# Seven block products for eight in the first MLP layer of the second pass

## The chip, the cores and the metric

The kernel runs on one core of a Trainium2 chip. The metric is device time in microseconds. A row or bar named PE is TensorE, DVE is VectorE, ACT is ScalarE, POOL is GpSimd and SP is the engine that issues nearly all transfers here.

## The reference

2048 tokens of width 640 are normalised, and two branches are added to the input: linear attention with a learned feature map (32 heads of 20), and an MLP that normalises once more.

```python
xn = _layernorm(x, axis=-1)
return x + _A_ref(xn, A_wqkv, A_w_phi, A_wo) + _B_ref(xn, B_w1, B_b1, B_w2, B_b2)

def _B_ref(x, w1, b1, w2, b2):
    y = _layernorm(x, axis=-1)
    h = _gelu(jnp.einsum("bsd,df->bsf", y, w1) + b1)      # 640 -> 1728
    return jnp.einsum("bsf,fd->bsd", h, w2) + b2          # 1728 -> 640
```

In the attention branch q and k go through a small matrix per head and two softmaxes (of p and of -p), `kv` and `z` are sums over all tokens, and the output is `(phi_q kv) / (phi_q z)`, projected by `wo`.

## The kernel before

Everything is float32. Each operand of a large product is split into a high part, which is the value rounded by a copy to `float32r`, and a low part, which is the rest. A product then takes three matmuls, high by high, high by low and low by high (`mm3`, lines 69 to 72). A split is one copy on ScalarE (line 61) and one subtraction on VectorE or POOL (line 64).

Activations lie turned: features on the 128 partitions, tokens along a row. The 2048 tokens are four blocks of 512. The 640 inputs are five slices of 128 (`KC`), the 1728 hidden features fourteen chunks of 128, the last one half full. Two chunks make a group `g`, seven groups in all.

The program has these stages on PE:

1. The first MLP pass, over blocks 0 and 1. Beside its matmuls a generator (`prep`) prepares the attention weights, and then normalises blocks 2 and 3 slice by slice and writes their high and low parts to DRAM (`y_dram`).
2. The projections of q, k and v for 16 tiles of 128 tokens, with the feature map on ScalarE, VectorE and POOL, and the sums `kv` on PE (to about 443 us of the trace).
3. The second MLP pass, over blocks 2 and 3, from there to about 648 us. Beside it a generator (`attend`) computes the attention output: it loads features `e`, splits them (ScalarE copy, POOL subtraction, lines 960 and 961), has PE multiply them with `kv` (lines 967 and 968), and puts the two halves of a bank together (lines 977 and 978). When a block is through, `quotients` brings the denominators into place and POOL multiplies by their reciprocals (line 1013).
4. The output projection, and its sum with the MLP result.

In a pass, `Mlp.passes(g, b, ws)` computes for a group and a block: for each of its two chunks five `mm3` into one PSUM bank (15 matmuls), gelu on ScalarE, high and low part of the result; then, after a `yield`, five rows of second products, each of two `mm3` into one of three banks, which VectorE adds to `acc[b]` (line 309). The second products of one group and block stand behind the first products of the next.

PE's order is written out by hand. What runs beside is interleaved by a call after each `mm3`, which advances the generator by one step:

```python
mm3(pz, w[0][:, kc, :], w[1][:, kc, :], y[b][0][:, kc, :], y[b][1][:, kc, :], kc == 0, kc == KC - 1)
next(self.beside, None)
```

In the second pass from group 1 on, the order on VectorE, ScalarE and POOL is the order of the program text too. Before that a scheduler sets it. An engine works through its queue in order, and a waiting instruction holds up those behind it. SP issues transfers in order in the same way.

The weights of a chunk are loaded to `r1` (of w1) and `r2` (of w2), split into one of four tiles `w0` to `w3`, and the next chunk is loaded when the split is through.

Of the kernel before, what the change touches and what calls it, by code (L numbers as in the profile page):

```python
# [51 lines left out]
def tile_kernel(ctx: ExitStack, tc: tile.TileContext, x, xT, wkT, wqT, wv, wphi, wo, w1, b1, w2, b2,  # L52
# [24 lines left out]
    ones1 = cp.tile([1, P], F32, name="ones1")  # L77
# [4 lines left out]
    rs_all = cp.tile([P, 16], F32, name="rs_all")  # L82
    nc.vector.memset(ones1, 1.0)
# [7 lines left out]
    r_dram = {n: tc.dram_tile([n, 8, P], F32, name=f"r{n}") for n in (1, 2)}  # L91
    a_dram = [tc.dram_tile([P, KC, 512], F32, name=f"a{b}") for b in range(2)]
# [108 lines left out]
    def load_rows(b):  # L201

        mr = mtile(5)
# [7 lines left out]
    class Mlp:  # L211
        def __init__(self, slots, hid):
            self.hid, self.turn, self.slots, self.beside, self.raw = hid, 0, slots, iter(()), {}
            self.ph, self.px, self.po = Banks(0, 1, 2), Banks(3, 4), Banks(5, 6, 7)

# [40 lines left out]
        def first(self, g, j, b, w, gt, hh, hl):  # L256
            pz = self.ph()
            for kc in range(KC):
                mm3(pz, w[0][:, kc, :], w[1][:, kc, :], y[b][0][:, kc, :], y[b][1][:, kc, :], kc == 0, kc == KC - 1)
                next(self.beside, None)  # L260
# [6 lines left out]
        def passes(self, g, b, ws, hid=None):  # L267
# [27 lines left out]
            for m in range(KC):  # L295
                pw = self.po()
                ms = slice(m * P, (m + 1) * P)
                for j, (hh, hl) in enumerate(hid):
                    w2h, w2l = ws[j][2:]
                    if hl is not None:  # L300
                        mm3(pw, w2h[:, ms], w2l[:, ms], hh, hl, j == 0, j == 1)
                        next(self.beside, None)
# [5 lines left out]
                else:  # L308
                    nc.vector.tensor_tensor(acc[b][:, m, :], pw, acc[b][:, m, :], op=ALU.add)  # L309

# [230 lines left out]
    def prep():  # L541
# [13 lines left out]
        mr = load_rows(2)  # L555
# [6 lines left out]


        def load(b, c):
            xc = fp.tile([P, D], F32, name="raw")[:, :512]
            nc.sync.dma_start(xc, xT[c * P:(c + 1) * P, b * 512:(b + 1) * 512])
            return xc

        for b in range(2, 4):
            ahead = load(b, 0)  # L570
            if b == 3:
                mr = load_rows(3)
            for _ in range(5 if b == 2 else 10):
                yield
            for c in range(KC):
                xc, ahead = ahead, load(b, c + 1) if c < KC - 1 else None
                nc.gpsimd.tensor_tensor(xc, xc, mr[:, 0], op=ALU.subtract)
                for _ in range(3):
                    yield
                nc.vector.tensor_tensor(xc, xc, mr[:, 1], op=ALU.mult)  # L580
                for _ in range(2):
                    yield
                hl = fp.tile([P, 2, KC, G5], F32R, name="t").rearrange("p a c f -> p a (c f)")[:, :, :512]
                nc.scalar.activation(hl[:, 0], xc, AF.Copy)
                for _ in range(2):
                    yield
                nc.vector.tensor_tensor(hl[:, 1], xc, f(hl[:, 0]), op=ALU.subtract)
                for p in range(2):
                    nc.sync.dma_start(y_dram[b - 2][p][:, c, :], f(hl[:, p]))
                yield  # L590
# [193 lines left out]
    for t, i in [(t, i) for t in range(14) for i in range(4)] + TAIL:  # L784
# [35 lines left out]
        if (t, i) == (11, 0):  # L820
            mlp = Mlp((0, 3, 2, 1), ((1, 2), (0, 3)))
            mlp.ph = ptile
            mlp.fetch(0)
        if (t, i) == (12, 3):
            with tc.issue_after(evac):
                ws = [mlp.take(0)]
            mlp.fetch(1)
        if (t, i) == (15, 3):
            w, late = mlp.take_parts(1)
            ws.append(w)  # L830
# [3 lines left out]
    mlp.fetch(2)  # L834
    wkv.close()

# [6 lines left out]
    kvs = bp.tile([P, 11, P], F32R, name="kvs")  # L843
    fs = ExitStack()
# [20 lines left out]
    load_acc(3)  # L865

# [10 lines left out]
    def finish_kv(pxt):  # L877
# [9 lines left out]
        def done(tp, dens, mask, hi, lo):  # L887
# [3 lines left out]
            km = sp.tile([G6, 5, VR], F32, name="km", bufs=2)[:r, :n, :w]  # L891
# [25 lines left out]
    class Attention:  # L917

        def __init__(self, b, bank):
            self.b, self.n, self.bank = b, 0, bank  # L920
            self.ob = op.tile([P, KC, 512], F32, name=f"ob{b}") if b < 2 else acc01.tile([P, KC, 512], F32, name=f"acc{b - 2}")
# [12 lines left out]
        def groups(self, wait, first, gaps, lag):  # L934
# [16 lines left out]
            for p in late:  # L951
                self.second(*p)
                yield
                yield

        def first(self, g):
# [4 lines left out]
            nc.gpsimd.tensor_tensor(pl, e, f(ph), op=ALU.subtract)  # L961
            return ph, pl

        def second(self, g, ph, pl):
# [13 lines left out]
            nc.vector.tensor_tensor(o, pn[a, :], t, op=ALU.add)  # L978
            if g == 10:
                nc.sync.dma_start(o_dram[self.b], o[0:40])  # L980
# [134 lines left out]
    for _ in before:  # L1115
        pass
# [83 lines left out]
```

## Time and profile before

| | |
|---|---|
| time, median of 3 runs | 721.05 us (720.82 to 721.19) |
| span of the profiled execution, from its first to its last instruction | 719.3 us |
| median less that span | 1.75 us |
| busy: PE, DVE, ACT, POOL | 710.7, 477.6, 323.0, 384.1 us |
| DMA | 91.88 MB, mean 128 GB/s |

The profile comes from one execution; the page gives its span, and the table the distance to the runs' median. Instructions that only wait or issue transfers are not counted as busy. PE's matmuls overlap, so that a row of 0.39 us can stand 0.23 us after the one before it. The name on the left of an arrow is the tile written, those on the right the tiles read. In brackets stands how long the engine was idle before, and what ended that.

### The profile page before, as it was taken

To read this page: it belongs to the slowest core of one execution; us is meant where nothing else is said; L and a number is where in the kernel's file an instruction comes from. 1 tells how busy PE (TensorE), PEld (TensorE's weight loads), DVE (VectorE), ACT (ScalarE), POOL (GpSimd) and SP (SyncE) were. 2 spreads that over 40 slices of the span, in tenths; PEclk is the share of its full clock that TensorE was granted. 3 is DMA by queue.
4 is the path that set the end of the run, shared out by engine and by line. 5 is a ranking of instruction groups with operands and counts; after the bars stand their busy time and mean duration, and the time that the engine had idled before them with its cause. 6 is when DMAs were issued, how large, how long until landed. Compare 5 with 4: busy or idle time off the path is not lost.

```text
span 719.3 us, 9640 instructions
## 1 busy us (share of the span) xinstructions
PE 710.7 (99%) x3411; PEld 598.2 (83%) x3411; DVE 477.6 (66%) x787; ACT 323.0 (45%) x530; POOL 384.1 (53%) x332
## 2 busy tenths in 40 slices
PE   8989999999999999999999999999999999999998
PEld 7868888888888888888888887888888888888887
DVE  7776754757554788788898887635565566766432
ACT  6434454334334544545435446346565556530200
POOL 3521223345045997897878879346577787403000
PEclk9999999999999999999999999999999999999999
DMA  9803642656411227326302506943443443164122
GB/s 328 264 8 109 195 133 84 179 158 192 139 74 73 92 82 232 85 97 214 80 0 55 130 3 204 229 144 111 135 128 127 134 153 94 49 230 132 74 87 74
DMA packets 60454, 91.88 MB, mean 128 GB/s; under 512 B 7014, under 2 KB 31366, under 8 KB 59038
## 3 DMA queue, kind: packets, MB, share of 16 engines
q1 hardware_dynamic: 60102, 91.25, 40.7%
q8 instruction: 27, 0.44, 0.2%
q14 instruction: 21, 0.17, 0.1%
q10 hardware_dynamic: 304, 0.01, 0.0%
HBM read 63.51 MB, written 27.73 MB: 127 GB/s over the span
## 4 chain that ended last, share of the span: by engine, by line
PE 87%; DVE 3%; POOL 3%; ACT 1%; issue 1%; DMA 0%; SPq 0%; POOLq 0%
PE bank L673 23%; PE bank L70 18%; PE bank L72 18%; PE bank L71 18%; PE bank L743 2%; PE bank L499 2%; POOL m L708 2%; PE bank L967 1%; PE bank L968 1%; POOL m L719 1%; PE bank L305 1%; PE bank L285 1%; PE bank L304 1%; PE bank L286 1%; DVE sm L711 1%
## 5 line engine op out<-in xcount | busy, mean ns | idle before, releaser
L673 PE MATMUL bank<-wkh,y 128*128 128x512 f32 (+1 forms) x480 | 139.5, 364 | 0.0
L64 POOL TENSOR_TENSOR w<-r,w 128x640 fp32r<-128x640 f32 x52 | 83.3, 1619 | 95.6 <-ACT w L61 64.7
L70 PE MATMUL bank<-y,w 128*128 128x512 f32 (+1 forms) x334 | 129.8, 389 | 1.0 <-ACT m L264 1.0
L71 PE MATMUL bank<-y,w 128*128 128x512 f32 (+1 forms) x334 | 129.2, 387 | 0.0
L72 PE MATMUL bank<-y,w 128*128 128x512 f32 (+1 forms) x334 | 129.2, 387 | 0.0
L70 PE MATMUL bank<-m,w 128*128 128x512 f32 x260 | 102.4, 394 | 2.6 <-DVE acc L309 2.3
L72 PE MATMUL bank<-m,w 128*128 128x512 f32 x260 | 101.3, 389 | 0.0
L71 PE MATMUL bank<-m,w 128*128 128x512 f32 x260 | 101.2, 389 | 0.0
L673 PEld LDWEIGHTS bank<-wkh,y 128*128 128x128 f32 x480 | 87.5, 188 | 13.3
L309 DVE TENSOR_TENSOR acc<-bank,acc 128x512 f32<-128x512 f32 x120 | 81.1, 684 | 19.8 <-PE bank L72 11.8
L673 PE MATMUL bank<-wkl,y 128*128 128x512 f32 (+1 forms) x240 | 87.4, 364 | 0.0
L64 DVE TENSOR_TENSOR m<-m,m 128x512 fp32r<-128x512 f32 (+1 forms) x54 | 43.7, 814 | 65.5 <-ACT m L61 65.3
L70 PEld LDWEIGHTS bank<-y,w 128*128 128x128 f32 x334 | 62.7, 188 | 13.9 <-ACT m L264 1.2
L72 PEld LDWEIGHTS bank<-y,w 128*128 128x128 f32 x334 | 62.7, 188 | 12.8
L71 PEld LDWEIGHTS bank<-y,w 128*128 128x128 f32 x334 | 62.7, 188 | 12.5
L264 ACT ACTIVATE m<-bank,b1t 128x512 f32<-128x512 f32 (+1 forms) x54 | 36.2, 671 | 65.2 <-PE bank L72 61.0
L709 ACT ACTIVATE m<-m,rs_all 128x1280 f32<-128x1280 f32 x32 | 43.7, 1365 | 42.9 <-POOL m L708 42.9
L70 PEld LDWEIGHTS bank<-m,w 128*128 128x128 f32 x260 | 48.8, 188 | 14.4 <-DVE acc L309 3.5
L961 POOL TENSOR_TENSOR e<-e,m 128x512 fp32r<-128x512 f32 x28 | 36.2, 1295 | 41.8 <-ACT m L960 35.8
L711 DVE TENSOR_REDUCE sm<-m 128x64 f32<-128x1280 f32 x32 | 47.4, 1481 | 15.5 <-ACT m L709 15.4
L673 PE MATMUL bank<-w,y 128*128 128x512 f32 x240 | 57.4, 391 | 0.0
L72 PEld LDWEIGHTS bank<-m,w 128*128 128x128 f32 x260 | 48.8, 188 | 10.3
(156 smaller groups left out, 1249.3 us busy)
## 6 DMA issues: line engine op xcount, KB each, us to landing
r<-in_w SPq DMA_DIRECT2D x52, 320.0 KB
e<-e SPq DMA_DIRECT2D x40, 256.0 KB
e<-acc SPq DMA_DIRECT2D x52, 160.0 KB
acc<-in_xT SPq DMA_DIRECT2D x4, 1280.0 KB
xb<-in_x SPq DMA_DIRECT2D x8, 320.0 KB
t<-in_x SPq DMA_DIRECT2D x8, 320.0 KB
raw<-in_xT SPq DMA_DIRECT2D x10, 256.0 KB
yh<-t SPq DMA_DIRECT2D x10, 256.0 KB
```

The source lines that it names most:

```text
L64: eng.tensor_tensor(lo, src, f(hi), op=ALU.subtract)
L70: nc.tensor.matmul(ps, lh, rh, start=first, stop=False, **kw)
L71: nc.tensor.matmul(ps, lh, rl, start=False, stop=False, **kw)
L72: nc.tensor.matmul(ps, ll, rh, start=False, stop=last, **kw)
L264: nc.scalar.activation(gt, pz, AF.Gelu_apprx_tanh, bias=b1t[:, 2 * g + j:2 * g + j + 1])
L309: nc.vector.tensor_tensor(acc[b][:, m, :], pw, acc[b][:, m, :], op=ALU.add)
L499: nc.tensor.matmul(ps[:, u * nh * DF:(u + 1) * nh * DF], raw[:nh * DH, u * P:(u + 1) * P], wpt[:nh * DH, g, :nh, 1:], start=True, stop=True)
L673: nc.tensor.matmul(ps, lh[:, kc, c], rh[:, kc], start=n == 0, stop=n == 3 * KC - 1)
L708: subs[n, t] = nc.gpsimd.tensor_tensor(ep[:, s], a, b, op=ALU.subtract)
L709: exps[n, t] = nc.scalar.activation(e, e, AF.Exp, scale=rs_all[:, t:t + 1])
L711: nc.vector.tensor_reduce(sm, e.rearrange("p s (h f) -> p (s h) f", f=DH), axis=AX, op=ALU.add)
L961: nc.gpsimd.tensor_tensor(pl, e, f(ph), op=ALU.subtract)
```

## The change

For groups 1 to 5 of the second pass, the first products of a pair of chunks and of blocks 2 and 3 are computed together. Two chunks by two slices on the left, and two slices by two blocks on the right, are a 2 x 2 by 2 x 2 product of blocks; Strassen's method in Winograd's form takes seven products instead of eight. Slices 0 and 1 are one such product, slices 2 and 3 the other; slice 4 is computed as before (`rest`). Groups 0 and 6 stay as they were.

The weights' sums (`s1`, `s2`, `s4`, and `s3` in the place of a21) are computed by POOL in float32 and split: the rows and `s` go through ScalarE; the low part of `s` is subtracted on VectorE. The sums and differences of blocks 2 and 3 are computed in `prep` during the first pass, on POOL, and stored to `t_dram`; `t2`, `t3` and `t4` come back to two tiles `tf`, and `t1` takes the place of slices 0 and 2 of block 3, `y[3]`. The products gather in three banks; the four results are copied out of a bank by ScalarE, and VectorE adds another bank to each.

```diff
+        def cross(self, g, bs, before, later):
...
+            product("a", "a11", "b11", True)
+            copy(z11, "a")
+            product("c", "a12", "b21", True)
+            rest("c", 0, b0)
+            add(z11, "c")
+            hidden(z11, 0, hid[0][0])
+            next(before)
+            later[0]()
+            product("b", "s1", "t1", True)
+            copy(z22, "b")
+            product("a", "s2", "t2")
+            copy(z12, "a")
+            next(before)
+            later[1]()
+            next(before)
+            product("a", "s3", "t3")
+            copy(z21, "a")
+            bank["c"] = banks.tile([P, 512], F32, name="bank2")
+            product("c", "a22", "t4", True)
+            rest("c", 1, b0)
+            add(z21, "c")
+            hidden(z21, 1, hid[0][1])
+            product("b", "s4", "b22")
+            rest("b", 0, b1)
+            add(z12, "b")
+            self.after(2, lambda: gelu(z12, 0))
+            next(before)
+            later[2]()
+            rest("a", 1, b1)
+            add(z22, "a")
+            self.after(2, lambda: gelu(z22, 1))
+            for _ in before:
+                pass
```

Here `product` is two `mm3` (slices 2q and 2q + 1 of a block), `next(before)` is one row of the second products of the group before, and `later` are the splits of this group's w2 and the sums of the next group's w1. The second products of block 2 follow, with the splits of the next group's w1 beside their first three rows.

The weights are now loaded and split in other pieces: both chunks of w1 of a group, then both of w2, through the same two tiles `r1` and `r2`.

```diff
+        def sums(self, g):
...
+            for out, x0, x1, op in ((s[:, 0], a21, a22, ALU.add), (a21, a11, a21, ALU.subtract),
+                                    (s[:, 1], s[:, 0], a11, ALU.subtract), (s[:, 2], a12, s[:, 1], ALU.subtract)):
+                nc.gpsimd.tensor_tensor(out, x0, x1, op=op)
```

Steps are put off. The call after each `mm3` is now `tick`, which first issues what has come due and then advances the generator. With it the low part of a weight or of `e` is issued one tick after its high part, the add of attention's two halves two ticks after the copy, and gelu two ticks after the add.

```diff
+        def tick(self):
+            self.ticks += 1
+            while self.due and self.due[0][0] <= self.ticks:
+                self.due.pop(0)[2]()
+            next(self.beside, None)
...
-            nc.gpsimd.tensor_tensor(pl, e, f(ph), op=ALU.subtract)
+            mlp.after(1, lambda: nc.gpsimd.tensor_tensor(pl, e, f(ph), op=ALU.subtract))
```

At the start of the second pass two loads of `tf` (1.6 MB each) and four loads of `t1` into `y[3]` are added; after group 5, slices 0 and 2 of `y[3]` are loaded again. Space is found by keeping the attention output of all blocks in the tiles `acc0` and `acc1`: blocks 0 and 1 are written to DRAM after the multiplication and loaded back for the output projection.

```diff
+    for q in range(2):
+        nc.sync.dma_start(f(tf[q]), t_dram[q][:, 1:4])
...
-            self.ob = op.tile([P, KC, 512], F32, name=f"ob{b}") if b < 2 else acc01.tile([P, KC, 512], F32, name=f"acc{b - 2}")
+            self.ob = acc01.tile([P, KC, 512], F32, name=f"acc{b % 2}")
...
+                    if self.b < 2:
+                        nc.sync.dma_start(ob_dram[self.b][:, c - 1], ob[:, c - 1])
```

A small constant tile is shortened, another (`pad`) added, and a scratch area shortened, so that the tiles that one instruction reads and writes start at the same address modulo 64.

More of the change, by code (lines that the diff above doesn't have):

```diff
@@ L1115, in tile_kernel @@
-    for _ in before:
-        pass
+    nothing = iter(())
+    mlp.beside = finish_kv(mlp.px)
+    with tc.issue_after(subs["q", 15].ins):
+        mlp.sums(1)
+    this = mlp.passes(0, 3, ws)
+    next(this)
+    finish(before)
+    before = this
+    for q in range(2):
+        for p in range(2):
+            nc.sync.dma_start(f(y[3][p][:, 2 * q]), t_dram[q][:, 0, p])
+    mlp.places()
+    for part in mlp.splits(1):
+        part()
+        mlp.tick()
+    mlp.tick()
+    mlp.fetch_pair(1, True)
@@ new lines, in tile_kernel @@
+    for g in range(1, 6):
+        w2t, later = gathered(g)
+        hid, more = mlp.cross(g, (2, 3), before, later)
+        if g < 5:
+            parts = mlp.splits(g + 1)
+        else:
+            w1t, parts = mlp.take_pair(6, False, 1)
+        for m, _ in enumerate(mlp.second(g, 2, w2t, hid[0])):
+            next(more, None)
+            if m < len(parts):
+                parts[m]()
+            if m == 3:
+                mlp.fetch_pair(g + 1, True)
+        before = mlp.second(g, 3, w2t, hid[1])
@@ L1119, in tile_kernel @@
+    finish(before)
     pw_ = Banks(6, 7)
```

301 lines of the change are left out of this document (220 added, 81 removed).

## The prediction

> **What bounds the kernel now.** I read the page first, then the busy time by stretches, then the second pass in order of time.
>
> ```profile
> PE 710.7 (99%) x3411; PEld 598.2 (83%) x3411; DVE 477.6 (66%) x787; ACT 323.0 (45%) x530; POOL 384.1 (53%) x332
> PEclk9999999999999999999999999999999999999999
> PE 87%; DVE 3%; POOL 3%; ACT 1%; issue 1%; DMA 0%; SPq 0%; POOLq 0%
> ```
>
> TensorE is busy for 99% of the span at a full granted clock, and the chain that ended last runs through it for 87%. The stretches show where it is not full:
>
> ```profile
> core 0: us, PE busy (x) PEld busy (x) DVE busy (x) ACT busy (x) POOL busy (x), PEclk, DMA share, GB/s
> 120.00:200.00 80.00, 80.00 (x353) 65.92 (x352) 49.50 (x67) 28.72 (x45) 30.23 (x21) 1.00 0.53 160
> 480.00:620.00 140.00, 140.00 (x619) 115.94 (x618) 84.50 (x141) 82.64 (x137) 96.00 (x72) 1.00 0.39 120
> 440.00:460.00 20.00, 19.00 (x112) 16.46 (x110) 15.80 (x25) 11.82 (x18) 15.93 (x15) 1.00 0.62 158
> ```
>
> In the second MLP pass (480 to 620) PE has no gap in 140 us, while POOL is busy for 69% and VectorE for 60%. So a matmul taken out there is worth its whole issue interval, as long as nobody makes PE wait. That interval:
>
> ```profile
> 500.18 0.39 PE L71 MATMUL bank<-m,w 128*128 128x512 f32 x1
> ...
> 514.00 0.39 PE L72 MATMUL bank<-y,w 128*128 128x512 f32 x1
> ```
>
> These are 61 matmuls apart in the listing, so 13.82 / 61 = 0.2266 us each; the 0.39 us of a row is pipelined.
>
> **What the change removes.** For each of the five pairs, the old first products take 2 chunks x 2 blocks x 5 slices x 3 = 60 matmuls. Seven products for each of two slice pairs, and four for the fifth slice, make (14 + 4) x 3 = 54. Nothing else on PE changes. The gain is 5 x 6 x 0.2266 = **6.80 us**. The one PE gap in this half is
>
> ```profile
> 443.40 0.50 PE L70 MATMUL bank<-y,w 128*128 128x512 f32 x1 [0.99 <-ACT m L264]
> ```
>
> It lies ahead of the first changed product, behind the same exp and gelu on ScalarE, so I leave it; if it went, 1.0 us more.
>
> **What it adds on ScalarE and VectorE.** Per pair: four copies out of PSUM and four adds out of PSUM.
>
> ```profile
> L690 ACT ACTIVATE m<-bank 128x512 f32<-128x512 f32 x16 | 10.0, 623 | 15.1 <-PE bank L673 10.5 <-issue 4.0 <-ACT w L61 0.6
> L309 DVE TENSOR_TENSOR acc<-bank,acc 128x512 f32<-128x512 f32 x120 | 81.1, 684 | 19.8 <-PE bank L72 11.8 <-PE bank L305 6.7
> L264 ACT ACTIVATE m<-bank,b1t 128x512 f32<-128x512 f32 x50 | 34.4, 688 | 64.8 <-PE bank L72 60.6 <-DVE m L64 2.5 <-DVE ra L158 0.9
> L61 ACT ACTIVATE m<-m 128x512 fp32r<-128x512 f32 x50 | 31.6, 632 | 1.6
> ```
>
> That is 4 x 0.62 = 2.5 us and 4 x 0.68 = 2.7 us in a pair of now 114 + some 18 attention matmuls = 132 x 0.2266 = 29.9 us. ScalarE goes from 59% to about 69%, VectorE from 60% to about 73% with the split of the sums. The tightest hand-over is z12: its copy must leave bank a before s3·t3 adds to it. Two rows of the pass before lie between, 12 matmuls and a pair = 3.2 us, and in that time ScalarE has about 1.8 us queued ahead and behind (two 0.6 us copies and the copy itself). The last hidden chunk, z21, has add, gelu, high part, low part = 0.68 + 0.69 + 0.63 + 0.69 = 2.7 us to do while PE has some 32 matmuls, 7 us. Both hold; I take nothing for them. The steps put off by ticks, and the new addresses, touch only these queues, whose spare 27 to 31% is the cover; without it their cost would be that of the late z12, below.
>
> **What it adds in the first pass.** Eight subtractions on POOL, eight high and low parts and eight more stores, spread over some 80 us. POOL is at 38%, ScalarE at 36% there (row of 120 to 200), DMA at 0.53. Covered: nothing, at most 0.5 us if a store holds up ScalarE. After the last pair y and two blocks of attention are loaded again, 3.6 MB or 12 us at the 301 GB/s quoted below; their first reader comes 85 matmuls or 19 us later: nothing, or up to 1 us.
>
> **What it adds on SP where the second pass begins.** This is one of two places where I expect a price. SP's queue there, before:
>
> ```order
> L226 DMA r_4160<-in_w 128x640
> L227 DMA r_4161<-in_w 128x640
> L776 DMA e_72<-acc_2000 32x10x128 x8
> L776 DMA e_72<-et 32x10x128 x4
> L776 DMA e_72<-acc_1999 32x10x128 x4
> L226 DMA r_4311<-in_w 128x640
> L227 DMA r_4312<-in_w 128x640
> ```
>
> Now, with `y` the two halves of block 3, `t` the stored differences and `e_73` the last features:
>
> ```order
> L1333 DMA y_3061<-t_86 128x512
> L1333 DMA y_3060<-t_86 128x512
> L998 DMA e_73<-acc_2045 32x10x128 x8
> L998 DMA e_73<-et 32x10x128 x4
> L998 DMA e_73<-acc_2044 32x10x128 x4
> L1333 DMA y_3060<-t_87 128x512
> L1333 DMA y_3061<-t_87 128x512
> L348 DMA r_4366<-in_w 128x640
> L348 DMA r_4367<-in_w 128x640
> ```
>
> The second two loads of y stand behind all sixteen stores. When do these end, and how full are the engines?
>
> ```profile
> 450.60 5.34 SPq L776 DMA_DIRECT2D e<-acc  x8
> ...
> 461.79 0.76 SPq L226 DMA_DIRECT2D r<-in_w  x1
> ...
> 452.00:462.00 10.00, 1.00 0.96 220
> 462.00:470.50 8.50, 1.00 0.99 301
> ...
> 462.32 0.39 PE L70 MATMUL bank<-y,w 128*128 128x512 f32 x1
> ```
>
> SP comes free at 461.8 and the engines are full until 470.5. With about 0.5 MB queued ahead (0.5 MB of early y loads went in before the stores) and 0.5 MB of their own at 301 GB/s, the loads end 3.5 us later plus a landing of 1 to 2 us: 466.3 to 467.3. PE starts the first changed group at 462.3 and needs them in the second half of s1·t1, behind 24 matmuls: 467.7. So 0 to 2.5 us; I take **0.5**.
>
> **What it adds on POOL.** Here is the other price. Durations (min/median/max):
>
> ```profile
> L64 POOL TENSOR_TENSOR w<-r,w x52: 1553/1572/2022, 8.8 to 603.6; 128x640 fp32r<-128x640 f32 x52
> L961 POOL TENSOR_TENSOR e<-e,m x28: 1282/1295/1315, 471.3 to 611.8; 128x512 fp32r<-128x512 f32 x28
> L1013 POOL TENSOR_TENSOR ob<-ob,rx x10: 1286/1308/1743, 531.4 to 580.6; 128x512 f32<-128x512 f32 x10
> L64 DVE TENSOR_TENSOR m<-m,m x54: 408/692/1784, 23.2 to 635.8; 128x512 fp32r<-128x512 f32 x50, 128x256 fp32r<-128x256 f32 x4
> L708 POOL TENSOR_TENSOR m<-m,mx 128x40 f32<-128x40 f32 x16 | 5.3, 330 | 0.0
> ```
>
> A pair now has four sums of 256 columns. They lie between the 40-column and the 512-column row, 0.33 to 1.295; I take half of the latter, 0.65, or 2.6 us a pair. And VectorE and POOL keep each other out:
>
> ```profile
> 595.69 0.69 DVE L64 TENSOR_TENSOR m<-m,m 128x512 fp32r<-128x512 f32 x1 [0.69 <-ACT m L61]
> 596.26 1.30 POOL L961 TENSOR_TENSOR e<-e,ph 128x512 fp32r<-128x512 f32 x1 [2.25 <-PE bank L967]
> ...
> 611.24 0.69 DVE L64 TENSOR_TENSOR m<-m,m 128x512 fp32r<-128x512 f32 x1 [0.75 <-ACT m L61]
> 611.81 1.30 POOL L961 TENSOR_TENSOR e<-e,m 128x512 fp32r<-128x512 f32 x1 [0.68 <-ACT m L960]
> ```
>
> Each time POOL's subtraction starts 0.57 us after a VectorE subtraction of two SBUF tiles, when that ends; and some of VectorE's take 1.78 instead of 0.69, behind one of POOL's. Five such VectorE instructions a pair (four hidden low parts, and the low part of the sums, 768 columns, about 1.0) hold POOL for 4 x 0.57 + 1.0 = 3.3 us. [...]
>
> In a pair with four of the five multiplications by the reciprocal denominators that is: nine e splits 11.7, four w splits 6.3, four sums 2.6, four multiplications 5.2, and 3.3 of lock = 29.1 of PE's 29.9 us; with eight e splits and no multiplication 22.6. So POOL is full in two stretches. Before, one of them (`e` a feature split, `w` weights, `ob` times `rx` the multiplication):
>
> ```order
> L1013 TENSOR_TENSOR ob_4335<-ob_4335,rx 128x512 x2
> L961 TENSOR_TENSOR e<-e,ph 128x512
> L64 TENSOR_TENSOR w_4985<-r_4854,w_4985 128x640
> L64 TENSOR_TENSOR w_4985<-r_4855,w_4985 128x640
> L1013 TENSOR_TENSOR ob_4335<-ob_4335,rx 128x512
> L961 TENSOR_TENSOR e<-e,m_4333 128x512
> ```
>
> Now, in the third of the five pairs:
>
> ```order
> L387 TENSOR_TENSOR w_4907<-r_4892,w_4907 128x640
> L1253 TENSOR_TENSOR acc_4392<-acc_4392,rx 128x512
> L1196 TENSOR_TENSOR e<-e,m_4390 128x512
> L1253 TENSOR_TENSOR acc_4392<-acc_4392,rx 128x512 x2
> L1196 TENSOR_TENSOR e<-e,m_4390 128x512
> L1253 TENSOR_TENSOR acc_4392<-acc_4392,rx 128x512
> L381 TENSOR_TENSOR s<-r_5013 128x256
> L381 TENSOR_TENSOR r_5013<-r_5012,r_5013 128x2x128
> L381 TENSOR_TENSOR s<-s,r_5012 128x256
> L381 TENSOR_TENSOR s<-r_5012,s 128x256
> L1196 TENSOR_TENSOR e<-e,ph 128x512
> ```
>
> Four sums have come between a multiplication and the e split that PE waits for. Measured from the start of that pair's second products for block 2: the copy behind the first row exists when s3·t3 starts, 45 matmuls earlier (-10.2), and POOL reaches it at about -9.7, behind an e split. Then 1.57 + 4 x 1.31 + 2 x 1.295 + 4 x 0.65 + 1.295 = 13.3 us, and two locks, 1.1: done at +4.7. PE asks at +3.4 (15 matmuls). PE waits **1.3 us** (0 to 2.5). An e split has had some 5 us to spare so far: POOL's ended at 518.8, PE's read started at 524.0.
>
> ```profile
> 517.52 1.29 POOL L961 TENSOR_TENSOR e<-e,m 128x512 fp32r<-128x512 f32 x1 [2.51 <-ACT m L960]
> 523.98 0.39 PE L968 MATMUL bank<-e,kvs 128*128 128x512 f32 x1
> ```
>
> Where the fourth pair passes to the fifth, multiplications of the second block meet sums and weight splits again; the same walk gives 2.0 us at an e split there, less if a lock falls into a gap: **1.5** (0 to 3.5).
>
> **The sum.** The profiled execution spans 719.3 us, the runs' median is 721.05; the 1.75 around the span stay. -6.80 + 0.5 + 1.3 + 1.5 = -3.5: a span of 715.8, a time of **717.6**.
>
> **The rivals.** *Nothing is lost:* POOL's gaps absorb the sums and the loads land in time. For it: PE had no gap in 140 us. Time 721.05 - 6.8 = 714.3. *All is given back at PSUM:* z12's copy or z21's chain comes late in every pair, since ScalarE takes its work in order and weight copies can wait there for a load. One row of six matmuls lost a pair, 5 x 1.36 = 6.8: 721.0. Against it: the slack of about 1.4 and 4 us. *Slower, POOL bounds the full pairs:* if a sum costs as much as 512 columns (1.295, +2.6 a pair), and the five meetings with VectorE cost POOL another 0.43 each (1743 against 1308), +2.2, such a pair needs 33.9 us against 29.9, and the queue never empties. Two full pairs and their neighbours, in which the backlog is not yet gone, give some 4 + 4 + 1 us, and 0.5 at the start: 721.05 - 6.8 + 9.5 = 723.8. It decides from 3.2 us over in each. [...] *The change doesn't do it:* the programs hold 3330 and 3300 matmuls, so it does.
>
> **How the numbers follow.** Forecast (715 to 719.5) 0.58, nothing lost 0.17, given back 0.11, slower 0.14. A difference under 0.2% (1.4 us) cannot be told from none here. So faster 0.75, same 0.11, slower 0.14. The range: down to nothing lost and a part of the 1.0 us gap, 713.8; up to all given back, 721.5.
>
> **What would show it.** PE busy about 30 x 0.2266 less; PE's waits naming POOL's e split in the third and the fourth to fifth pair; a wait of PE for a DMA of y near 467; copies of 0.62 and adds of 0.69 without a wait of PE behind them. Wrong if PE waits at every pair for a bank, or if sums take over 1 us.

## The result, and the profile after

The changed kernel takes 738.8 us (median of 4 runs, 736.9 to 740.3) where the kernel before takes 721.0: a ratio of 1.0246, 95% interval 1.023 to 1.0262. The forecast was 717.6, with 721.5 as the upper end. The profiled execution took 739.13 us, with a span of 737.3 (before: 719.3).

The page, busy time and instructions, granted clock, DMA traffic and the chain that ended last:

```profile
PE 713.9 (97%) x3381; PEld 594.6 (81%) x3381; DVE 518.3 (70%) x820; ACT 342.2 (46%) x563; POOL 423.0 (57%) x360
PEclk9999999999999999999999999999999998999999
DMA packets 65767, 106.56 MB, mean 145 GB/s; under 512 B 7462, under 2 KB 31814, under 8 KB 63838
PE 82%; DVE 5%; POOL 4%; DMA 4%; issue 2%; ACT 2%; SPq 0%; POOLq 0%; ACTq 0%; DVEq 0%
```

TensorE has 30 records less (3411 before), as the prediction says, and yet more busy time. Other engines and DMA have taken 5 points of the chain. The busy time by stretches shows where, first of the kernel before, then of the changed one:

```profile
230.00:430.00 200.00, 200.00 (x1036) 173.27 (x1035) 167.01 (x246) 99.00 (x154) 164.10 (x163) 1.00 0.33 96
580.00:620.00 40.00, 40.00 (x178) 33.14 (x177) 26.67 (x46) 22.64 (x38) 28.81 (x22) 1.00 0.28 88
```
```profile
230.00:430.00 200.00, 200.00 (x1021) 171.08 (x1020) 165.69 (x242) 98.11 (x151) 161.49 (x162) 1.00 0.32 96
540.00:580.00 40.00, 36.65 (x159) 29.47 (x158) 29.04 (x41) 24.20 (x40) 33.22 (x28) 1.00 0.49 153
580.00:620.00 40.00, 34.23 (x141) 27.17 (x140) 22.88 (x35) 17.80 (x30) 24.71 (x18) 0.96 0.69 221
620.00:660.00 40.00, 35.77 (x146) 28.96 (x147) 32.37 (x53) 25.12 (x44) 23.39 (x16) 0.91 0.44 150
```

Three things are to be seen. From 540 to 660 us PE is idle for 13.4 us and issues 446 matmuls in 120 us; at the 178 of the row before in 40 us it would be 534. In two of these stretches the granted clock is under 1 (0.96 and 0.91). And from 230 to 430, in the projections, which the change does not touch, PE is busy all the time, but 1021 matmuls fit where 1036 did: each takes longer.

PE's own waits in the second pass, by line, with the sum, the times and the longest:

```profile
PE bank L70 <- DVE acc L336: 7.1, 1, 7.1
PE bank L1202 <- DVE acc L1216: 2.4, 2, 2.2
PE bank L70 <- ACT m L443: 2.1, 2, 1.8
PE bank L1203 <- POOL e L1196: 1.6, 1, 1.6
PE bank L70 <- ACT m L280: 0.8, 1, 0.8
PE bank L70 <- DVE acc L325: 0.8, 1, 0.8
```

The wait for L280 stands where the pass begins, and the kernel before has it too (1.0 us). The longest, in order of time (what else ran then is left out):

```profile
609.40 1.85 SPq L1164 DMA_DIRECT2D e<-e  x1
609.58 0.67 DVE L1216 TENSOR_TENSOR ts<-bank,ts 42x512 f32<-42x512 f32 x1
...
611.76 0.43 SPq L1376 DMA_DIRECT2D tf<-ob  x1
612.29 0.35 SPq L1218 DMA_DIRECT2D o<-ts  x1
612.68 0.27 SPq L1219 DMA_DIRECT2D d<-ts  x1
...
616.01 0.39 PE L72 MATMUL bank<-m,w 128*128 128x512 f32 x1
...
621.50 0.59 ACT L1212 ACTIVATE ts<-bank 64x512 f32<-64x512 f32 x1 [10.41 <-DMA d<-ts]
622.13 0.68 DVE L1216 TENSOR_TENSOR acc<-bank,ts 64x512 f32<-64x512 f32 x1 [10.14 <-ACT ts L1212]
622.74 0.67 DVE L336 TENSOR_TENSOR acc<-bank,acc 128x512 f32<-128x512 f32 x1
623.31 1.28 POOL L1196 TENSOR_TENSOR e<-e,ph 128x512 fp32r<-128x512 f32 x1 [12.87 <-ACT ph L1195]
623.46 0.80 PE L70 MATMUL bank<-m,w 128*128 128x512 f32 x1 [7.07 <-DVE acc L336]
624.06 0.63 PE L71 MATMUL bank<-m,w 128*128 128x512 f32 x1
624.49 0.63 PE L72 MATMUL bank<-m,w 128*128 128x512 f32 x1
```

This is attention's group 10, the denominators. Its sum stays in `ts`, from which two transfers take it to DRAM. The next copy into `ts` (L1212) must wait for both. They were issued 2.7 and 3.1 us behind the start of the sum, since SP had other transfers ahead: a load of `e`, for which SP itself waited 1.8 us on a matmul, and last the reload of `ob`. The second had landed only 8.8 us later, among reloads that filled the transfer engines (share 0.96 from 610 to 620). The same transfer, issued at 525.67 and 567.08 us, had landed after 2.2 us each time, at shares of 0.67 and 0.30 in those 2.2 us. No run moves the reloads, so their part in the 8.8 us is read from the trace and not tested. ScalarE stood for 10.4 us at the head of its queue, VectorE behind it for 10.1, POOL for 12.9, and PE for 7.1 us once its banks were full. Then it ran at 0.43 us a matmul instead of 0.23. The tile `ts` in both traces, what the engine waited for before touching it (before, then after):

```profile
  DMA o<-ts: 5.1, 2
  DMA d<-ts: 1.1, 1
```
```profile
  DMA d<-ts: 20.3, 3
```

The whole difference adds up from the starts of PE's rows. The second pass begins 3.1 us later (443.40 and 446.50). From there on: pauses of over 0.6 us from one matmul's start to the next, 15.1 us beyond the usual interval (before: none); intervals of 0.25 to 0.6 us, mostly the slow matmuls behind pauses, 5.1 (before: 0.55); the small rest on each interval, 1.9; less 30 x 0.2266 = 6.8. Together 3.1 + 15.1 + 4.5 (5.1 less 0.55) + 1.9 - 6.8 = 17.8; the last matmul starts 17.8 us later (715.81 and 733.64).

### The profile page after: what moved, and what is told of

It is laid out like the page before. It is cut to its first block, busy times and chain, and to the rows that moved or that the text cites. A ratio compares the mean times of both kernels' runs of the same rounds, so it can differ in the third digit from the quotient of the medians.

```text
span 737.3 us, 9741 instructions
## 1 busy us (share of the span) xinstructions
PE 713.9 (97%) x3381; PEld 594.6 (81%) x3381; DVE 518.3 (70%) x820; ACT 342.2 (46%) x563; POOL 423.0 (57%) x360
## 4 chain that ended last, share of the span: by engine, by line
PE 82%; DVE 5%; POOL 4%; DMA 4%; issue 2%; ACT 2%; SPq 0%; POOLq 0%; ACTq 0%; DVEq 0%
PE bank L895 27%; PE bank L70 15%; PE bank L71 15%; PE bank L72 15%; PE bank L965 2%; PE bank L693 2%; DMA d<-ts 1%; POOL e L1196 1%; POOL w L387 1%; PE bank L1203 1%; PE bank L1202 1%; DMA t<-t 1%; POOL acc L1253 1%; DVE m L455 1%; DMA r<-sr 1%
## 5 line engine op out<-in xcount | busy, mean ns | idle before, releaser
L895 PE MATMUL bank<-wkh,y 128*128 128x512 f32 (+1 forms) x480 | 141.1, 367 | 0.0
L70 PE MATMUL bank<-y,w 128*128 128x512 f32 (+1 forms) x294 | 115.0, 391 | 0.8 <-ACT m L280 0.8
L70 PE MATMUL bank<-m,w 128*128 128x512 f32 x260 | 104.0, 400 | 11.4 <-DVE acc L336 7.1
L72 PE MATMUL bank<-y,w 128*128 128x512 f32 (+1 forms) x294 | 114.3, 389 | 0.0
L71 PE MATMUL bank<-y,w 128*128 128x512 f32 (+1 forms) x294 | 114.2, 389 | 0.0
L64 POOL TENSOR_TENSOR w<-r,w 128x640 fp32r<-128x640 f32 x32 | 53.5, 1684 | 98.8 <-ACT w L61 68.0
L71 PE MATMUL bank<-m,w 128*128 128x512 f32 x260 | 102.2, 393 | 0.0
L72 PE MATMUL bank<-m,w 128*128 128x512 f32 x260 | 102.1, 393 | 0.0
L70 PEld LDWEIGHTS bank<-m,w 128*128 128x128 f32 x260 | 49.5, 190 | 24.7 <-DVE acc L336 7.5
L70 PEld LDWEIGHTS bank<-y,w 128*128 128x128 f32 x294 | 55.5, 189 | 12.4 <-ACT m L280 1.0
L72 PEld LDWEIGHTS bank<-y,w 128*128 128x128 f32 x294 | 55.5, 189 | 11.6
L71 PEld LDWEIGHTS bank<-y,w 128*128 128x128 f32 x294 | 55.6, 189 | 11.2
L72 PEld LDWEIGHTS bank<-m,w 128*128 128x128 f32 x260 | 49.3, 190 | 10.7
L71 PEld LDWEIGHTS bank<-m,w 128*128 128x128 f32 x260 | 49.4, 190 | 10.0
L930 POOL TENSOR_TENSOR m<-m,mx 128x640 f32<-128x640 f32 (+2 forms) x48 | 44.4, 938 | 19.5 <-DVE mx L919 19.5
L325 DVE TENSOR_TENSOR acc<-bank,acc 128x512 f32<-128x512 f32 x70 | 47.0, 683 | 12.0 <-PE bank L321 6.2
L1212 ACT ACTIVATE ts<-bank 64x512 f32<-64x512 f32 (+1 forms) x44 | 26.1, 593 | 56.3 <-PE bank L1203 35.6
```

The lines of the kernel that those rows point to most:

```text
L64: eng.tensor_tensor(lo, src, f(hi), op=ALU.subtract)
L70: nc.tensor.matmul(ps, lh, rh, start=first, stop=False, **kw)
L71: nc.tensor.matmul(ps, lh, rl, start=False, stop=False, **kw)
L72: nc.tensor.matmul(ps, ll, rh, start=False, stop=last, **kw)
L895: nc.tensor.matmul(ps, lh[:, kc, c], rh[:, kc], start=n == 0, stop=n == 3 * KC - 1)
L930: subs[n, t] = nc.gpsimd.tensor_tensor(ep[:, s], a, b, op=ALU.subtract)
```

## The experiments

Each stands beside runs of the kernel before on the same chip, whose median was 720.9 or 721.0 us every time. Lines are those of the changed kernel unless said; an added line moves those below by one.

### The addresses

Two edits of one line: more padding among the constants moves all tiles that lie at the low end of SBUF (`y`, `w`, `m`, `r`, `s`), and none of those at the high end (`wkh`, `wkl`, `kvs`, `tf`, `e`). In the kernel before the same line is added:

```diff
-    cp.tile([P, 8], F32, name="pad")
+    cp.tile([P, 24], F32, name="pad")     # alike128; [P, 56] in alike256
```
```diff
     rs_all = cp.tile([P, 16], F32, name="rs_all")
+    cp.tile([P, 16], F32, name="pad")     # before_shifted
```

> The changed kernel with 64 bytes more of padding among its constants, so that every tile that pools place from the low end of SBUF moves by 64 bytes and all operands of 512-column matmuls are alike mod 128, not only mod 64. Theory A (part of the loss is that the changed addresses make each matmul slower whose moving operand differs by 64 from its weights mod 128): in the trace of after such matmuls follow each other at 233.2 ns in the middle stage, where alike ones take 228.4, and 480 of wkh/wkl and 90 of tf are of the kind; 570 x 5 to 6.5 ns = 2.9 to 3.7 us less, about 735.6. The second pass begins at about 440.6 to 442 in the trace, not 445.4. Rival B (the slower spacing of that stretch is the chip or the clock of that run): 738.8, no change.

> The kernel before, with 64 bytes of padding among its constants and nothing else: its operands then stay alike mod 64, and 480 matmuls of wkh and wkl and 28 of kvs have a moving operand that differs from its weights by 64 mod 128. Theory A (alike mod 128 counts): 480 to 508 x 4.8 to 5.6 ns = 2.3 to 2.8 us slower, about 723.6, and the spacing in the middle stage is 233 instead of 228 ns. Rival B (only mod 64 counts, or the spacing is the chip's): 721.0, no change.

> The changed kernel with 192 bytes more of padding among its constants: moving operand and weights of every 512-column matmul are then alike mod 256, as in the kernel before. The padding of 64 bytes left the middle stage at 231.6 ns a matmul (before: 228.3); by the rows of that run, matmuls whose two operands differ by 128 or 384 mod 512 take up to 236.7, those alike mod 256 229. Theory A (alike mod 256 counts): the middle stage goes back to 228.3 ns, from 206.6 to 204.3 us, and the second pass from 229.4 to about 227 ns a matmul outside its stalls, some 850 x 2.4 ns = 2.0 us: 738.8 - 4.3 = about 734.5, with the long stalls still there. Rival B (which address counts is something else): the middle stage stays at 206.5 us, and the time is that of the 64-byte padding, 735.0, or of the change.

Measured: 735.05 us with 64 bytes (ratio 1.0195, 1.0177 to 1.0212), 732.35 with 192 bytes (1.0168, 1.0149 to 1.0186), and 724.42 for the shifted kernel before (1.0049, 1.0036 to 1.0061). In the projections, with the distance of `wkh` from `y00` that the program gives, and the length from the first to the last of the 480 matmuls that stream 512 columns of `wkh` or `wkl`:

```
kernel             (wkh - y00) mod 512   matmuls 230-430 us   length, us
before                       0                 1036             204.24
before, shifted            448                 1023             206.63
changed                    448                 1021             206.63
changed, 64 B              384                 1023             206.46
changed, 192 B             256                 1036             204.24
```

The row of the changed kernel with 192 bytes is that of the kernel before again:

```profile
230.00:430.00 200.00, 200.00 (x1036) 173.28 (x1035) 167.02 (x246) 99.04 (x154) 164.15 (x163) 1.00 0.33 96
```

Alike mod 64, which the change provides, is not what counts here, nor mod 128: at 384 the stage is as slow as at 448. At 0 and 256 it is fast. Matmul by matmul (intervals under 0.25 us), in the stage of the run with 64 bytes, those whose operands are 0 apart mod 512 took 229.1 ns, those 384 apart 236.3, and those 128 apart, which alternate with these, 229.4; which of two neighbours causes the delay can't be told from this. So my first theory fell in its modulus and stood in its kind; that the time came near its 735.6 was luck. The time that the 64 bytes seemed to gain (3.7 us) was not the stage's, which stayed at 206.5 us. One stall in the first pass, 1.0 us, happened not to occur, and the pauses of the second pass were 1.5 us shorter. Alike mod 256 gives the whole 2.4 us of the stage back, and in the second pass the small rest on each interval falls from 1.9 to 0.2 us in all. The gain, 6.4 us, is 2.1 more than expected: in the profiled run the stall of the first pass is missing here too, and the pauses of the second pass are 1.6 us shorter. The kernel before, shifted, shows both parts without any stall: 2.4 us in the projections and 1.3 in the second pass.

### The tile `ts` and the putting-off

```diff
+            self.od = ep.tile([P, 512], F32, name="od")
...
-                t = o = self.ts[a, :]
+                t = o = self.od[a, :]          # own_tile: group 10 alone
```
```diff
-            mlp.after(2, whole)
+            mlp.after(1, whole)                # one_tick; whole() in sum_at_once
```

> The changed kernel with a tile of its own (od) for the result of attention group 10, which the changed kernel keeps in ts until two transfers have read it. Theory A (the three long stalls of the second pass, at 528, 568 and 616 us of the trace, are ScalarE waiting to write ts while the transfers of the group 10 before it read it; VectorE, GpSimd and then TensorE stand behind that): the stalls of 0.4 + 2.0 + 7.2 us go, and with the longest one the slow matmuls behind it, 10 x 0.2 = 2.2 us, and half of the smaller ones that follow: 11 to 14 us less, about 726; no wait of ts for a DMA of d is left. Rival B (GpSimd is the bound of the full pairs, and ScalarE's wait only hides that it would wait there for GpSimd): the waits move to GpSimd's splits of e and the time falls by under 4 us, above 734.8.

> Both edits: the padding and the own tile of group 10. If the two costs are independent: the two savings add, 738.8 - 3.3 - 12.5 = about 723. What then is left against the 714.2 that the removed matmuls alone would give, some 9 us, is that of GpSimd's and VectorE's queues (stalls at 550 and 591 us of the trace of after, 1.7 and 2.3 us, with 2.0 of slow matmuls behind the second), and smaller ones. Rival: they overlap, and the sum is above 726.

> The own tile of group 10 and the 192 bytes of padding. If the address cost adds to the rest: 726.5 of the own tile with the 64-byte padding, less 2.2 in the middle stage and 2.1 in the second pass = about 722.2. If stalls take up what faster matmuls give (the other engines are then the bound): 724.5, the middle stage's part alone.

> As the kernel with own tile and 192 bytes, and the sum of an attention group's halves put off by one tick instead of two. Theory A (TensorE's stall of 2.4 us near 586 us is that sum, which waits on VectorE behind a subtraction that GpSimd's split stretched from 0.7 to 1.9 us, while it holds the bank that the next group needs): the sum goes ahead of that subtraction, the stall shrinks to under 0.7 us: about 2 us less than the kernel it is made from, 720. Rival (VectorE and GpSimd have more to do there than TensorE leaves time for): the wait moves to another step, no change within 0.7 us.

> The changed kernel with one part undone: the sum of an attention group's two halves is issued right behind its copy, as in the kernel before, and not put off by two ticks; ts is shared and the addresses are the changed ones. Theory A (the putting-off made the transfers out of ts start some 3.3 us later, which is the wait of ScalarE, and kept the bank of the group from TensorE): the waits of ts for a DMA fall to under 3 us in all, as before the change, and of the loss the address part (4.5 us) and a few stalls of GpSimd are left: 738.8 - 14 = about 725. Rival B (VectorE now waits at each of the 44 sums for ScalarE's copy of 0.6 us, and the copies and low parts of the hidden chunks behind it come late): under 5 us gained, above 733.

> The changed kernel with the sum put off by one tick and nothing else. With the sum at once it was 732.04, with two ticks 738.8. Theory A (two ticks hold the bank and start the transfers too late, none makes VectorE wait for ScalarE at each sum): one tick is the best of the three, about 729. Rival (the later the worse, in step): 735.5.

> The changed kernel with the 192 bytes of padding and the sum put off by one tick, ts still shared: against the padding alone (732.35) it is the tick's part without the own tile, against the best kernel (718.92) the own tile's part with one tick. Theory A (both the late start of the transfers out of ts and the shared tile count): the wait of ts shrinks but stays where the reloads run, near 612 us: about 725. Rival B (the two ticks alone were at fault, with one the transfers are through in time): 719 to 720, and the own tile is worth nothing.

> The best kernel so far (own tile, operands alike mod 256, sum put off by one tick) with the sum at once. Theory A (the sooner the bank is given back the better): the two stalls near 586 us, 0.5 + 0.8, lose the first: 718.4. Rival (VectorE waits in its queue for the copy): 719 to 721.

Measured, medians in us, with the ratio to the kernel before and its interval:

```
                                  two ticks                     one tick                      at once
shared ts, changed addresses      738.8  1.0246 (1.023-1.0262)  728.3   1.0098 (1.0075-1.0121)  732.04  1.0155 (1.0142-1.0168)
shared ts, alike 256              732.35 1.0168 (1.0149-1.0186) 723.98  1.0039 (1.0025-1.0054)  -
own tile, changed addresses       727.91 1.0092 (1.0076-1.0107) -                               -
own tile, 64 B                    726.52 1.0091 (1.0075-1.0108) -                               -
own tile, alike 256               726.19 1.0091 (1.007-1.0113)  718.92  0.9979 (0.9969-0.9989)  723.0   1.0028 (1.0017-1.0039)
```

The own tile alone gives 10.9 us, just under theory A's 11 to 14 and far from its rival's 4, and no wait of the copies for a transfer is left. But a wait of PE of 4.1 us remains, of another kind. In the kernel with own tile and 192 bytes it is 3.4 us:

```profile
615.80 0.01 DVE L1252 LOAD_MASK_SELECT rx<-rx  x1 [3.40 <-DMA rx<-d]
615.82 0.72 DVE L1252 STREAM_SHUFFLE rx<-rx 128x512 f32<-128x512 f32 x1
616.44 0.67 DVE L336 TENSOR_TENSOR acc<-bank,acc 128x512 f32<-128x512 f32 x1
...
617.03 1.40 DVE L455 TENSOR_TENSOR m<-m,m 128x512 fp32r<-128x512 f32 x1
...
618.46 0.69 DVE L1217 TENSOR_TENSOR acc<-bank,ts 64x512 f32<-64x512 f32 x1
...
619.21 0.80 PE L1203 MATMUL bank<-m,kvs 128*128 128x512 f32 x1 [3.39 <-DVE acc L1217]
```

Here L1217 is the put-off sum. PE has two banks for attention, and the next product but one needs the bank that this sum reads. A shuffle whose reciprocals have not landed, a row's sum and a low part stand ahead of it, all because it was put off. With one tick it stands ahead of the shuffle, and the wait is gone: 726.19 to 718.92, 7.3 us for a step moved by three matmuls (0.68 us). Between the two profiled runs pauses shrink by 3.3 us, and the slow matmuls behind them by 3.4. That is more than theory A's 2 us, and not at its place: at 586 us PE waited for a split of e in both runs (1.2 us, then 0.6 beside 0.4 for the sum). The other side is VectorE's wait for ScalarE's copy ahead of each sum: between 440 and 660 us it is 5.4 us with two ticks, 18.2 with one and 25.1 with none (own tile, alike 256). At none it costs more than it saves, 723.0, worse than either theory of that run had it. One tick is best in both rows where all three were run; that the later the worse, the rival there, fell.

With `ts` shared and changed addresses, ScalarE's wait for the transfers out of it is 20.3 us with two ticks, 8.0 with one (longest 6.3) and 10.8 with none; theory A of the sum at once had said under 3 and 725 us, and its rival over 733, so that run lies between. Near 610 us, where the reloads run, the copy waits for the transfers with one tick and with none too (6.3 and 6.0 us). So the tile and the tick are two costs: the own tile is worth 5.1 us with one tick and 6.2 with two (alike 256). Cure by cure from the changed kernel the gains are 6.4 (addresses), 10.9 (tile) and 10.5 us (tick), 27.8 together; all three give 19.9. So they overlap: the stalls that each of them cures are in part the same. The pair "own tile, 64 B" points the same way, with 12.3 instead of the 14.6 of its parts, and its rival (above 726) was right. Own tile with 192 bytes came to 726.19, where 722.2 was expected, or 724.5 if stalls took up the gain. In the profiled runs the stage gained its 2.2 us over the 64 bytes, but the pause near 616 grew from 3.4 to 3.8 us from start to start, and was now followed by twelve slow matmuls.

### The queues of POOL and VectorE

From the kernel with own tile, 192 bytes and one tick ("best", 718.92 us), four edits spread other work:

```diff
-            for i in range(6):                               # shuffles_later
+            for i in range(12 if self.b == 2 else 6):
...
-                for i in range(3):                           # products_apart
+                for i in range(4 if self.b < 2 else 3):
```
```diff
-                nc.gpsimd.tensor_tensor(out, x0, x1, op=op)  # sums_apart
+                step = partial(nc.gpsimd.tensor_tensor, out, x0, x1, op=op)
+                step() if g == 1 or not i else self.after(2 * i, step)
```
```diff
             at[0].split(c, nc.vector)                       # splits_spread
-            if c % 2:
-                yield
+            yield
+            yield
```

> As the run before it, and the five shuffles and multiplications of the third batch begin 12 ticks instead of 6 behind their last load. Theory A (the stall of 3.2 us near 620 us is VectorE at the head of its queue with a shuffle whose input is late, since the small loads share the transfer engines with the reloads of 3.6 MB): the stall goes, 3 us less, about 717; that would be under the kernel before by 0.5%. Rival: the shuffles then meet the split of the last weights, and under 1 us is gained.

> The best kernel so far with the multiplications by the reciprocals four ticks apart instead of three in the first two batches. Theory A (the stalls left, 1.1 us at 545 and 0.5 + 0.8 us at 586, are GpSimd's queue: a multiplication of 1.3 to 2.2 us stands ahead of a split of e that the next product waits for): about 1.5 us less, 717.4. Rival (the four sums of the next pair ahead of that split are the cause at 545, and VectorE at 586): no change within 0.7 us.

> The best kernel so far with the four sums of the next pair's blocks issued two ticks apart instead of in one block of 2.9 us on GpSimd. Theory A (that block is ahead of a split of e in the third pair, the prediction's term of 1.3 us): the stall of 1.1 us at 545 goes, 717.8. Rival (GpSimd has no room there anyway): the stall moves to the multiplication or the split of weights behind, no change within 0.5 us.

> The best kernel so far with the six steps of the first output's split two ticks apart instead of two steps to a tick. Theory A (the stall of 1.0 us near 636 us, and 1.6 to 3.2 us in the runs that shift other work, is VectorE with four or five subtractions of this split in a row, 3.4 to 4.3 us, ahead of the low part of a hidden chunk that TensorE waits for): the stall goes, 1 us less in a run like the profiled one, 717.9, and less spread. Rival (they start when the reload has landed, whatever their ticks): no change within 0.5.

> The best kernel so far with the split spread, the multiplications four ticks apart and the four sums two ticks apart. In the two runs that spread the multiplications or the sums the stall at 545 us was gone, but that near 636 us was 2.0 us with 1.6 us of slow matmuls behind it. Theory A (these are separate waits): with that one out of the way too, 718.92 - 1.1 - 1.0 = 716.8. Rival (VectorE and GpSimd are full in this stretch, and each wait that goes comes back elsewhere): 718 to 722.

Measured: shuffles later 722.8 us (1.0025, 1.0013 to 1.0036), products apart 721.89 (0.9999, 0.9984 to 1.0013; 717.5 to 723.6 over 12 runs), sums apart 719.78 (0.9989, 0.9974 to 1.0003), splits spread 718.53 (0.9969, 0.9957 to 0.9981), the last three together 717.28 (0.9957, 0.9944 to 0.9969). The twelve runs of products apart fall in two groups: five of 717.5 to 719.8 us with a granted clock of 0.999 or 1.0, and seven of 721.8 to 723.6 us with 0.997 or 0.998, the profiled one among these, in which slow matmuls follow a pause of 2.2 us. PE's waits in the second pass, without the 1.0 us where it begins: the best kernel, sums apart, and all spread (whose lines are numbered one or two higher):

```profile
PE bank L1204 <- POOL e L1197: 1.5, 2, 0.9
PE bank L70 <- DVE acc L325: 0.8, 1, 0.8
PE bank L1203 <- DVE acc L1217: 0.4, 1, 0.4
```
```profile
PE bank L71 <- DVE acc L326: 1.8, 1, 1.8
PE bank L1205 <- DVE acc L1219: 0.8, 1, 0.8
PE bank L1206 <- POOL e L1199: 0.5, 1, 0.5
```
```profile
PE bank L71 <- DVE acc L337: 0.6, 1, 0.6
PE bank L1206 <- POOL e L1199: 0.6, 1, 0.6
PE bank L1205 <- DVE acc L1219: 0.2, 1, 0.2
```

The first kernel waits for a split of e twice, near 546 and 587 us. With the sums or the products apart the one at 546 is gone: POOL's queue there is the one that the prediction walked through, and either of the two steps that stand ahead of the split can be moved. The wait for L326, near 637 us, grows instead, from 0.8 to 1.8 or 1.9 us: it stands behind five subtractions of the first output's split in a row on VectorE (4.3 us in both, 3.9 in the best kernel). That also undid the later shuffles: the stall that they were to cure was gone with the single tick, and they only pushed more work into that stretch (a pause of 3.4 us instead of 1.2 there, and seven slow matmuls). With the split spread the wait is gone in the profiled run, as theory A said, but the median moved by 0.4 us only, the number of its rival. The rival's reason did not hold, since the subtractions do lie apart in the trace; that run's second pass began 0.75 us later, behind a stall in the first pass, which took up most of the gain. All three together were expected at 716.8 and measured at 717.28. So these are separate waits for the most part, and not a limit of VectorE or POOL.

## Why the prediction was wrong

Its sum was -6.80 + 0.5 + 1.3 + 1.5. By its steps:

- **The removal, -6.80.** It held in the count (3411 and 3381 records). The account of the trace takes it as given, so its closing is no proof of the price; that comes with the mended kernels, which end below the kernel before.
- **The start of the second pass, +0.5.** It was 0: no wait of PE stands near 467 us. That the pass begins 3.1 us late has other causes, below.
- **POOL in the third pair, +1.3.** Place, releaser and mechanism were right: PE waits at 552.48 for a split of e, 1.56 us, behind four sums of 0.73 to 0.74 each (taken as 0.65) and the multiplications. That the size came out too, 1.56 for 1.3, is in part luck: the sums took 0.3 us more than said, and where two locks of 0.57 were taken, one split of e took 0.45 more than the usual 1.30 (1.75 us at 545.17).
- **From the fourth to the fifth pair, +1.5.** The place was right, and the pause was 2.3 us beyond the usual interval, with 1.7 of slow matmuls behind it. The releaser was not a split of e but attention's sum on VectorE, behind a low part that POOL's split held up:

```profile
590.82 1.56 POOL L387 TENSOR_TENSOR w<-r,w 128x640 fp32r<-128x640 f32 x1
591.00 1.93 DVE L455 TENSOR_TENSOR m<-m,m 128x512 fp32r<-128x512 f32 x1
592.86 0.67 DVE L1216 TENSOR_TENSOR acc<-bank,ts 64x512 f32<-64x512 f32 x1
593.58 0.50 PE L1202 MATMUL bank<-m,kvs 128*128 128x512 f32 x1 [2.16 <-DVE acc L1216]
```

- **The lock, 0.57 us a meeting and 3.3 us a pair.** No run shows this term. The prediction took the 0.57 us from the start of a VectorE subtraction to that of POOL's split of e for time in which VectorE keeps POOL out. In the rows that it shows, ScalarE's copy of e, which the split reads, stands in between:

```profile
595.57 0.62 ACT L960 ACTIVATE ph<-e 128x512 fp32r<-128x512 f32 x1
611.12 0.62 ACT L960 ACTIVATE m<-e 128x512 fp32r<-128x512 f32 x1
```

  POOL's two splits, at 596.26 and 611.81, each start 0.08 us after that copy ends. Most of the 3.3 us of lock a pair thus stood on a wrong reading of the rows. That VectorE and POOL do hold each other up shows in rows that grow when they meet: above, VectorE's low part takes 1.93 instead of 0.69, and a multiplication on POOL from 592.33 takes 1.74 instead of 1.30. This was charged to POOL alone; VectorE pays as well. Its 20 low parts of the hidden chunks took 1.14 us each on the mean (0.69 was taken), and the low part of the sums 1.80 instead of 1.0:

```profile
L455 DVE TENSOR_TENSOR m<-m,m 128x512 fp32r<-128x512 f32 x20 | 22.8, 1140 | 1.1 <-ACT m L452 0.9
L387 DVE TENSOR_TENSOR w<-s,w 128x768 fp32r<-128x768 f32 x5 | 9.0, 1798 | 1.9 <-ACT w L386 1.9
```

- **"The steps put off by ticks, and the new addresses, touch only these queues, whose spare 27 to 31% is the cover".** This is the step that failed: it put both at nothing. The second tick of the put-off sum cost 10.5 us by itself and 7.3 with tile and addresses mended. The addresses cost 6.4 us (two ticks), 4.3 (one) and 1.7 (two, own tile); 2.4 in the projections and 1.7 in the second pass are their own, and the rest goes with the stalls. That the spare time of an engine covers a put-off step was wrong in kind: what counts is what stands ahead of the step in its queue, and who waits for its bank or its tile.
- **The reloads, "nothing, or up to 1 us".** Their own reader was not late, as the prediction says. But two small transfers that a copy waits for shared SP's queue and the transfer engines with them, and the second took 8.8 us to land. A tile of its own for these transfers' source gave 10.9 us. A buffer that is written again, `ts`, was named nowhere, though the trace of before had its waits: 6.2 us in 3.
- **The first pass, 0 to 0.5.** One stall of 1.0 us beyond the interval (at 156 us), not in every run.
- **The copies and adds at nothing.** In the changed kernel PE waits twice for such a copy, that of z12 out of bank a: 1.8 us directly behind a wait for `ts`, and 0.4. With the own tile, and in every run with one tick or none, this wait is gone, so the term held by itself.
- **The rivals.** The slower one (723.8) had the right sign, and not the mechanism: the sums took 0.74 us, not 1.295, and the full pairs were no longer bound by POOL once the tile, the tick and the addresses were mended. "All is given back at PSUM" had PE late in every pair; it waited for z12's copy in two places. No rival had a tile that can't be written again before a transfer out of it is through.

With the three mended and the work spread, the kernel takes 717.28 us, 0.43% under the kernel before. So the seven products do pay: of the 6.8 us, 3.6 arrive. The rest is in pauses (1.6 us in the profiled run of this kernel), intervals of 0.25 to 0.6 us (0.9 beyond those of before) and a second pass that begins 0.3 us later. That this is close to the forecast of 717.6 says nothing for the forecast, which was for the kernel without these edits.

## What to carry to other kernels

When a step is put off, or a tile kept longer, list for each buffer who writes it next and what stands ahead of that step and behind it in its queue; an engine's spare share says nothing on that. A transfer that a buffer waits for should not share its issuing queue and its moment with large loads: here one took 8.8 us to land among them and 2.2 us elsewhere, though no run moves the loads. When a change moves tiles, look at the spacing of matmuls in a stage that the change doesn't touch: here it showed what the addresses cost there, 2.4 us. And before calling a delay a lock, look for the operand that came last.

## What the runs showed of the hardware

**Addresses.** The interval of 512-column matmuls grew where moving operand and weights were 128 and 384, or 192 and 448 bytes apart mod 512, by 1.1 to 1.2% over the projections (204.24 to 206.5 or 206.6 us), with PE busy all the time and a granted clock of 1.00. At 0 and 256 it did not (204.24 us at both). Why is not shown.

**Slow matmuls behind a pause.** In the second passes of the changed kernel and of its fifteen variants, no pause under 2.1 us (from start to start) was followed by a row of slow matmuls; of 20 longer ones, 2.2 to 7.5 us, 14 were, by five to twelve at 0.427 us each, which is a cost of 1.5 to 2.8 us on top. Six, of 2.2 to 3.4 us, were not. In the changed kernel the granted clock was 0.50 from 593.98 to 597.39 us and from 621.29 to 628.11, which is where its slow matmuls lie, behind pauses of 2.55 and 7.45 us, and 1.00 in the rest of the second pass, also behind a pause of 2.19 us that ended at 570.50. Pauses of 2.2 to 2.6 us were followed by slow matmuls in four cases. Why pauses of like length were followed by them in one place and not in another is not shown.
